# The output projection of a gated expert layer as seven block products instead of eight

## The chip, the cores and the metric

The kernel runs on one core of a Trainium2 chip. The metric is device time in microseconds (us), the median over several executions; beside it stands one profiled execution, whose trace the rows below are taken from.

## The reference, cut to what matters

Windowed attention (4 batches, 8 heads, 512 local and 32 global tokens, head size 64) gives 2176 token rows of 512 features. Two expert layers follow, and the change is in the last matrix product of the second:

```python
def _moe_ref(x, w1, w2, w3, w_out):
    h = np.maximum(np.maximum(x @ w1, x @ w2), x @ w3)
    return (h @ w_out).astype(np.float32)

def _moe2_ref(x, w_gate, w_val, w_out):       # x 2176 x 512, w_gate and w_val 512 x 1536
    gate = 1.0 / (1.0 + np.exp(-(x @ w_gate)))
    val = x @ w_val
    return (gate * val @ w_out).astype(np.float32)   # w_out 1536 x 512
```

## The kernel before, in words

**Stages.** The first 400 us are attention with the first expert layer woven in. From about 450 to 697 us the products x @ w_gate and x @ w_val run ("layer 3"), and from 697 us to the end the product with w_out ("layer 4").

**Number format.** Each f32 operand of layers 3 and 4 is split into a high half (rounded by a cast on ACT) and a low half (the rest, a subtraction on DVE). A product is the sum of three matmuls, high x high, high x low and low x high (`TERMS`), so each pair of 128-row blocks costs three matmuls on PE, each with its own weight load.

**Layer 3** already works with seven products instead of eight. For each gate or value matrix, each pair of 128 output columns (`j`) and each of three groups of tokens (`PAIRS`, twice 384, 384 or 320 tokens) there is a unit of seven products, `l3_prod(u, k)`. Products 1, 6, 7 and 4 add into one PSUM bank ("a"), with copies of it taken by ACT between them (`snap`); products 5 and 3 share a second bank ("e"), product 2 has a third ("b"). `l3_out` adds a bank and a copy on DVE. The order on PE is 1, 5, (4 of the unit before), 6, 2, (3 of the unit before), 7, so the copies have time while PE does another product. The gated result goes to DRAM as `gd`, feature blocks by tokens, through SP's DMA queue (L1051).

**Layer 4.** `wo_pre` (six times during layer 3) loads two 128-row blocks of w_out, brings them to f32 and stores them in DRAM (`wod`). Near the end of layer 3, as places in SBUF come free, `wo_prep` loads the twelve blocks and splits them. `g_prep(i)` loads the 1536 x 128 block of `gd` for token tile i (768 KB) and splits it in two pieces of 768 columns, a cast (L1089) and a subtraction (L1091) each. `moe2_l4(i, f)` issues the 12 x 3 matmuls of 512 columns of tile i into one bank, with the tokens' block as the stationary operand (L1102), and `moe2_out` copies the bank out and stores it. There are 17 tiles, 612 matmuls. Tile 0 runs before products 4 and 3 of the last layer 3 unit (the two "leftover" products), tiles 1 to 16 after them.

**Order.** Each step is a generator; every `yield` is a place where other work may stand. All steps are numbered events, and the list `ORDER` at the head of the file says in which order they are issued. Each engine, and SP's queue of DMA issues, takes its own instructions strictly in that order; the framework adds the waits. Places in SBUF are given by hand (`mem(at, ...)`), so a load into a place waits until what was there has been used.

## Time and profile before

| what | us |
|---|---|
| median of 3 runs | 845.67 (844.76 to 848.22) |
| the profiled execution | 843.73 |
| its span, first to last instruction | 842.0 |
| tile 0 of layer 4 on the chain | 697.85 to 706.04 |
| tiles 1 to 16 of layer 4 on the chain | 707.79 to 838.39 |

PE is TensorE's matmuls, PEld its weight loads (they overlap matmuls), DVE is VectorE, ACT ScalarE, POOL GpSimd, SPq the queue of DMA issues. L1102 is line 1102 of the kernel. In a row of a group, "x612 | 139.1, 389" means 612 instructions, 139.1 us busy in union, 389 ns from start to end of one; matmuls are pipelined, so the spacing of their starts is less than that length. "[0.35 <-ACT sn L1030]" means that the engine was idle for 0.35 us before, until that instruction.

### The profile page before, as it was taken

The page shows a single profiled execution, that of the slowest core. Times are in us where ns is not written, and L with a number is a line of the kernel's source. Part 1 is how long each engine was busy: PE and PEld are TensorE (multiplying, and loading weights), DVE is VectorE, ACT ScalarE, POOL GpSimd, SP SyncE. Part 2 cuts the span into 40 slices and gives each one's busy share as a digit, 9 for nine tenths or more (in the row PEclk, how much of TensorE's full clock was granted, in tenths as well). Part 3 has the DMA queues.
Part 4 walks back from the last instruction along what each step waited for, and adds up shares of the span by engine and source line. Part 5 has one row for each costly group of instructions (what it writes and reads, how often), then busy time and mean ns, then how long its engine had stood idle before and what let it go on. Part 6 is the DMA issues. An engine that isn't in the chain of part 4 may idle for free.

```text
span 842.0 us, 17071 instructions
## 1 busy us (share of the span) xinstructions
PE 815.9 (97%) x6422; PEld 744.4 (88%) x6422; DVE 529.8 (63%) x1200; ACT 452.1 (54%) x1112; POOL 148.5 (18%) x149
## 2 busy tenths in 40 slices
PE   6899699999999999999999999999999999999998
PEld 4678589898999988899999999999999998888886
DVE  3979767756676666864686887867766575222210
ACT  4986466746555565564456656556655453222220
POOL 3142245334232332323220000000000000000000
PEclk9999899999999999999999999999999999999999
DMA  9977346544453455444435244646442286445320
GB/s 208 273 182 190 86 79 115 88 88 97 95 108 80 78 114 104 89 94 82 153 124 191 97 159 144 223 153 192 164 146 77 72 256 196 130 122 147 108 70 37
DMA packets 224706, 109.72 MB, mean 130 GB/s; under 512 B 160752, under 2 KB 209392, under 8 KB 224624
## 3 DMA queue, kind: packets, MB, share of 16 engines
q1 hardware_dynamic: 221968, 107.98, 48.6%
q8 instruction: 50, 0.82, 0.4%
q10 hardware_dynamic: 2656, 0.66, 0.4%
q14 instruction: 32, 0.26, 0.1%
HBM read 71.76 MB, written 25.43 MB: 115 GB/s over the span
## 4 chain that ended last, share of the span: by engine, by line
PE 85%; DVE 5%; DMA 4%; SPq 2%; ACT 2%; issue 1%; POOL 0%; POOLq 0%; DVEq 0%; ACTq 0%
PE pa L1024 17%; PE acc L1102 16%; PE ps L320 10%; PE ps L322 9%; PE ps L321 9%; PE pe L1024 8%; PE pb L1024 4%; PE sp L612 3%; PE ot L766 2%; PE ps L904 2%; PE sg L629 1%; DMA m<-in_moe_w_dram 1%; DMA m<-in_v_l_dram 1%; PE ps L868 1%; PE og L835 1%
## 5 line engine op out<-in xcount | busy, mean ns | idle before, releaser
L1024 PE MATMUL pa<-m,m 128*128 128x384 f32 (+1 forms) x864 | 155.1, 327 | 0.3 <-ACT sn L1030 0.3
L320 PE MATMUL ps<-xt,m 128*128 128x288 f32 (+1 forms) x504 | 149.1, 296 | 2.1 <-DVE h L882 1.9
L322 PE MATMUL ps<-xt,m 128*128 128x288 f32 (+1 forms) x504 | 146.8, 291 | 0.0
L1024 PEld LDWEIGHTS pa<-m,m 128*128 128x128 f32 x864 | 144.4, 188 | 0.9 <-ACT sn L1030 0.8
L321 PE MATMUL ps<-xt,m 128*128 128x288 f32 (+1 forms) x504 | 144.9, 288 | 0.0
L1102 PE MATMUL acc<-m,m 128*128 128x512 f32 x612 | 139.1, 389 | 0.0
L1102 PEld LDWEIGHTS acc<-m,m 128*128 128x128 f32 x612 | 114.8, 188 | 23.7
L320 PEld LDWEIGHTS ps<-xt,m 128*128 128x128 f32 x504 | 94.7, 188 | 10.0 <-issue 4.3
L321 PEld LDWEIGHTS ps<-xt,m 128*128 128x128 f32 x504 | 94.8, 188 | 0.0
L322 PEld LDWEIGHTS ps<-xt,m 128*128 128x128 f32 x504 | 94.6, 188 | 0.0
L1091 DVE TENSOR_TENSOR m<-m,m 128x768 fp32r<-128x768 f32 x34 | 32.4, 958 | 87.5 <-ACT m L1089 87.5
L1030 ACT COPY sn<-pa 128x384 f32<-128x384 f32 (+1 forms) x108 | 49.7, 461 | 64.8 <-PE pa L1024 64.7
L1024 PE MATMUL pe<-m,m 128*128 128x384 f32 (+1 forms) x432 | 83.1, 327 | 0.0
L1089 ACT CAST m<-m 128x768 fp32r<-128x768 f32 x34 | 28.5, 840 | 83.9 <-PE acc L1102 71.7
L1024 PEld LDWEIGHTS pe<-m,m 128*128 128x128 f32 x432 | 72.8, 188 | 0.3 <-DVE m L1006 0.3
L647 ACT ACTIVATE sm<-sm,st 128x224 f32<-128x224 f32 x128 | 60.9, 479 | 11.0 <-DVE st L618 10.9
L882 DVE TENSOR_TENSOR h<-ps,h 128x288 f32<-128x288 f32 (+1 forms) x90 | 39.0, 437 | 43.6 <-PE ps L322 36.7
L270 POOL TENSOR_TENSOR h<-h,h 128x288 fp32r<-128x288 f32 (+1 forms) x42 | 41.4, 988 | 97.1 <-ACT h L887 93.1
L693 DVE TENSOR_TENSOR pc<-sm,pc 64x512 f16<-64x512 f32 (+1 forms) x72 | 51.8, 719 | 6.6 <-ACT pc L690 5.7
L618 DVE CUSTOM_DVE_ANT_0 sm<-sp,mask 128x224 f32<-128x224 f32 x128 | 43.8, 385 | 12.5 <-PE sp L612 9.8
L320 PE MATMUL ps<-h,m 128*128 128x288 f32 (+1 forms) x168 | 50.4, 300 | 0.0
L321 PE MATMUL ps<-h,m 128*128 128x288 f32 (+1 forms) x168 | 48.5, 289 | 0.6 <-POOL h L270 0.6
(162 smaller groups left out, 1436.0 us busy)
## 6 DMA issues: line engine op xcount, KB each, us to landing
m<-gd SPq DMA_DIRECT2D x17, 768.0 KB, 5.1
m<-in_moe_w_dram SPq DMA_DIRECT2D x18, 512.0 KB, 5.9
gd<-sgt SPq DMA_DIRECT2D x48, 192.0 KB, 1.9
m<-in_moe_w_val_dram SPq DMA_DIRECT2D x6, 1024.0 KB, 5.2
wr<-in_moe_w_out_dram SPq DMA_DIRECT2D x6, 1024.0 KB, 6.5
m<-in_moe_w_gate_dram SPq DMA_DIRECT2D x5, 1024.0 KB, 5.1
vr<-in_v_l_dram SPq DMA_DIRECT2D x48, 96.0 KB, 2.4
out_dram<-m SPq DMA_DIRECT2D x17, 256.0 KB, 2.4
```

The costliest lines, as they stand in the source:

```text
L270: nc.gpsimd.tensor_tensor(out=out, in0=a, in1=f32(b), op=ALU.subtract)
L320: nc.tensor.matmul(ps, lhsT=wh, rhs=xh, start=first, stop=False)
L321: nc.tensor.matmul(ps, lhsT=wh, rhs=xl, start=False, stop=False)
L322: nc.tensor.matmul(ps, lhsT=wl, rhs=xh, start=False, stop=last)
L618: nc.vector.tensor_tensor_reduce(out=sm[:, hh, j], in0=sp[hh][:, j, 0:224], in1=mask[:, half + j, :], scale=-SC, scalar=3.0e38, op0=ALU.ad ...
L647: nc.scalar.activation(sm4[:, i], sm4[:, i], AF.Exp, bias=st[:, 0, i:i + 1], scale=-1.0, accum_out=st[:, 2, i:i + 1])
L693: nc.vector.tensor_tensor(out=l_, in0=s_, in1=h_, op=ALU.subtract)
L882: nc.vector.tensor_tensor(out=a, in0=ps[:, 0:n], in1=a, op=ALU.max)
L1024: nc.tensor.matmul(ps, lhsT=w[l][:, a, i], rhs=x[m][:, i], start=(k in (1, 2, 5) and i + l + m == 0), stop=(k in (2, 3, 4) and i == 1 and ...
L1030: nc.scalar.copy(t[:, 0:n], pend[u]["a"][:, 0:n])
L1091: nc.vector.tensor_tensor(out=lo, in0=a, in1=f32(hi), op=ALU.subtract)
L1102: nc.tensor.matmul(acc[i], lhsT=t[l][:, f % 6], rhs=w[m], start=(f == 0 and l + m == 0), stop=(f == NF2 - 1 and l == 1))
```

## The change

Tile 0 (tokens 0 to 127) stays as it is, 36 matmuls of 512 columns. The other 2048 tokens are taken in 8 blocks of 256. A block's operand is four quarters (A11, A12, A21, A22: first or second half of the 1536 features by first or second 128 tokens), and w_out is four quarters of 768 x 256 (B11, B12, B21, B22). Seven products replace eight, with the sums S1 = A21 + A22, S2 = S1 - A11, S3 = A11 - A21, S4 = A12 - S2 on the tokens' side and T1 = B12 - B11, T2 = B22 - T1, T3 = B22 - B12, T4 = B21 - T2 on the weights'. Each product is 6 x 3 matmuls of 256 columns (`l4_prod`). Banks, copies, the order of the products and the output sums are those of layer 3 (`snap4`, `out4`), over the same PSUM tiles; in the last block 7 stands before the 3 of the block before.

`wo_pre` now loads one 128-row block of each half of w_out, makes the four sums (four subtractions of 256 columns on DVE) and stores them in DRAM (`wot`, two stores more). At the end of layer 3, `wo_prep` loads and splits the plain weights in six pieces of 1024 columns, and `wt_prep` the sums in four of 1536 columns. `g_first` loads and splits tile 0 in two halves. `g_prep(i)` loads 1536 x 256 of `gd` (1.5 MB, into one of three places), makes four sums of 768 columns on DVE and seven casts and seven low halves of 768 columns; for the halves of each of the seven operands there is one place, which all blocks share. `out4` makes three sums of 256 columns on DVE and one copy on ACT for each block, each with a store of 128 KB.

The new `ORDER` is the same up to the first event of layer 3. Around the first tile it has, on DVE: low half of tile 0's first half, low A11 of block 0 as the tile starts, the layer 3 outputs that are ready, low half of tile 0's second half, S1, S3, S2, low S1, low T4, low T3 (while tile 0 and the leftover products run), the last layer 3 outputs, low S2 (during product 1 of block 0), low A12, low S3, low A11 of block 1, low A22, S4 of block 0, S1 of block 1, low S4, S3 and S2 of block 1, an output sum, low S1 of block 1. On ACT, the casts stand in the same order, those of T4 and T3 between the casts of S1 and S2 of block 0. On SP's queue: three loads of plain weights (512 KB each), T2, two more loads of plain weights, tile 0's first half, block 0, tile 0's second half, and with the last products of layer 3 T4, T3 and block 1, with the stores of `gd` between.

```diff
@@ ORDER, lines 114 to 194 @@
...
@@ -261,7 +261,8 @@
     dram = ctx.enter_context(tc.tile_pool(name="dram", bufs=1, space=bass.MemoryType.DRAM))
     x2d = [dram.tile([KD, P, NT], F32, tag="x2d", name="x2d")]
     gd = dram.tile([NF2, P, NT], F32, tag="gd", name="gd")
-    wod = dram.tile([NF2, P, DM], F32, tag="wod", name="wod")
+    wod = dram.tile([P, 2, NF2 // 2, DM], F32, tag="wod", name="wod")
+    wot = dram.tile([P, 4, NF2 // 2, 256], F32, tag="wot", name="wot")
 
     def f32(ap):
         return ap.bitcast(F32)
@@ -1052,61 +1053,183 @@
         yield
 
     wo = {}
+    AJ, AT = (R0, R0 + 6144), (R0 + 12288, 7168, 0, 18432)
+    AGR, AO = (10240, 21504), 6144
+    AG = {A11: 16384, S1: 14848, S2: 13312, A12: 24576, S3: 3072, A22: 4608, S4: R0 + 15360}
 
     def wo_pre(i):
+
         raw = sg_pool.tile([P, 2 * DM, 2], I32, tag="wr", name="wr", bufs=1)
-        nc.sync.dma_start(out=raw.rearrange("p (f d) t -> p f (d t)", f=2),
-                          in_=w_out2[2 * i * P:(2 * i + 2) * P, :].rearrange("(f p) d -> p f d", p=P))
+        nc.sync.dma_start(out=raw.rearrange("p (h d) t -> p h (d t)", h=2),
+                          in_=w_out2.rearrange("(h f p) d -> f p h d", h=2, p=P)[i])
         yield
         c = mem(AST, (2 * DM,), I32)
         yield from to_f32(raw, True, out=c)
         yield
-        nc.sync.dma_start(out=wod[2 * i:2 * i + 2].rearrange("f p d -> p f d"), in_=f32(c).rearrange("p (f d) -> p f d", f=2))
-        yield
-
-    def wo_prep(f):
-        at = R0 + 1024 * f if f < 10 else AO2 + 1024 * (f - 10)
-        v = mem(at + DM, (DM,))
-        nc.sync.dma_start(out=v, in_=wod[f])
-        yield
-        hi = mem(at, (DM,), F32R)
+        c = f32(c).rearrange("p (h d) -> p h d", h=2)
+        nc.sync.dma_start(out=wod[:, 0:2, i], in_=c)
+        b11, b12, b21, b22 = c[:, 0, 0:256], c[:, 0, 256:512], c[:, 1, 0:256], c[:, 1, 256:512]
+        t12, t34 = mem(R0 - 8704, (2, 256)), mem(R0 - 512, (2, 256))
+        tt = nc.vector.tensor_tensor
+        tt(out=t12[:, 0], in0=b12, in1=b11, op=ALU.subtract)
+        yield
+        tt(out=t12[:, 1], in0=b22, in1=t12[:, 0], op=ALU.subtract)
+        yield
+        tt(out=t34[:, 0], in0=b22, in1=b12, op=ALU.subtract)
+        yield
+        tt(out=t34[:, 1], in0=b21, in1=t12[:, 1], op=ALU.subtract)
+        yield
+        for n, t in enumerate((t12, t34)):
+            nc.sync.dma_start(out=wot[:, 2 * n:2 * n + 2, i], in_=t)
+        yield
+
+    def split(at, src, n):
+
+        v = mem(at[1], (n,))
+        nc.sync.dma_start(out=v, in_=src)
+        yield
+        hi = mem(at[0], (n,), F32R)
         nc.scalar.copy(hi, v)
         yield
-        lo = mem(at + DM, (DM,), F32R)
+        lo = mem(at[1], (n,), F32R)
         nc.vector.tensor_tensor(out=lo, in0=v, in1=f32(hi), op=ALU.subtract)
-        wo[f] = hi, lo
-        yield
+        return hi, lo
+
+    def wo_prep(h, j):
+        at = AJ[h] + 1024 * j
+        v = yield from split((at, at + 3072), wod[:, h, 2 * j:2 * j + 2].rearrange("p f d -> p (f d)"), 1024)
+        wo[h, j] = [x.rearrange("p (f d) -> p f d", f=2) for x in v]
+        yield
+
+    def wt_prep(n):
+        v = yield from split((AT[n], AT[n] + 1536), wot[:, n].rearrange("p f d -> p (f d)"), 1536)
+        wo[(T1, T2, T3, T4)[n]] = [x.rearrange("p (f d) -> p f d", f=6) for x in v]
+        yield
+
+    def wo_op(op, f, m):
+
+        if op in wo:
+            return wo[op][m][:, f]
+        h, d = {B11: (0, 0), B21: (1, 0), B22: (1, 1)}[op]
+        return wo[h, f // 2][m][:, f % 2, 256 * d:256 * d + 256]
 
     gt = {}
 
+    def g_first(h):
+
+        raw = mem(AG[(S2, S1)[h]], (6, P))
+        nc.sync.dma_start(out=raw, in_=gd[6 * h:6 * h + 6, :, 0:P].rearrange("f p t -> p f t"))
+        yield
+        if h == 0:
+            t = sg_pool.tile([P, 2, 6, P], F32R, tag="wr", name="g0", bufs=1)
+        else:
+            t = mem(AG[S2], (2, 6, P), F32R)
+        nc.scalar.copy(t[:, 0], raw)
+        yield
+        nc.vector.tensor_tensor(out=t[:, 1], in0=raw, in1=f32(t[:, 0]), op=ALU.subtract)
+        gt[h] = t
+        yield
+
     def g_prep(i):
-        raw = mem(AXR + 1536 * (i % 2), (NF2, P))
-        nc.sync.dma_start(out=raw, in_=gd[:, :, i * P:(i + 1) * P].rearrange("f p t -> p f t"))
-        yield
-        for h in range(2):
-            a = raw[:, 6 * h:6 * h + 6]
-            hi, lo = (mem(7168 + 3072 * (i % 3) + 1536 * h + 768 * m, (6, P), F32R) for m in range(2))
-            nc.scalar.copy(hi, a)
-            yield
-            nc.vector.tensor_tensor(out=lo, in0=a, in1=f32(hi), op=ALU.subtract)
-            gt[i, h] = hi, lo
-            yield
+
+        if i % 3 < 2:
+            raw = mem(AGR[i % 3], (NF2, 2, P))
+        else:
+            raw = sg_pool.tile([P, 2, NT], F32, tag="sgt", name="graw", bufs=1).rearrange("p a t -> p (a t)")
+            raw = raw[:, 0:NF2 * 2 * P].rearrange("p (f h t) -> p f h t", f=NF2, h=2)
+        t0 = P + 256 * i
+        nc.sync.dma_start(out=raw.rearrange("p f h t -> p f (h t)"), in_=gd[:, :, t0:t0 + 256].rearrange("f p t -> p f t"))
+        yield
+        a11, a12, a21, a22 = raw[:, 0:6, 0], raw[:, 6:12, 0], raw[:, 0:6, 1], raw[:, 6:12, 1]
+        tt = nc.vector.tensor_tensor
+        s1 = mem(AG[S1] + 768, (6, P))
+        src = {A11: a11, S1: s1, S2: a11, A12: a12, S3: a21, A22: a22, S4: a22}
+
+        def high(op):
+            hi = mem(AG[op], (6, P), F32R)
+            nc.scalar.copy(hi, src[op])
+            gt[i, op] = hi, mem(AG[op] + 768, (6, P), F32R)
+
+        def lows(op):
+            hi, lo = gt[i, op]
+            tt(out=lo, in0=src[op], in1=f32(hi), op=ALU.subtract)
+
+        high(A11)
+        yield
+        lows(A11)
+        yield
+        tt(out=s1, in0=a21, in1=a22, op=ALU.add)
+        yield
+        high(S1)
+        tt(out=a21, in0=a11, in1=a21, op=ALU.subtract)
+        yield
+        tt(out=a11, in0=s1, in1=a11, op=ALU.subtract)
+        yield
+        lows(S1)
+        yield
+        for op in (S2, A12, S3, A22):
+            high(op)
+            yield
+            lows(op)
+            yield
+        tt(out=a22, in0=a12, in1=a11, op=ALU.subtract)
+        yield
+        high(S4)
+        yield
+        lows(S4)
+        yield
 
     acc = {}
 
-    def moe2_l4(i, f):
+    def l4_first(f):
         if f == 0:
-            acc[i] = ps_mm.tile([P, DM], F32, tag="mm", name="acc")
-        t, w = gt[i, f // 6], wo[f]
+            acc[0] = ps_mm.tile([P, DM], F32, tag="mm", name="acc")
+        t, w = gt[f // 6], wo[f // 6, f % 6 // 2]
         for l, m in TERMS:
-            nc.tensor.matmul(acc[i], lhsT=t[l][:, f % 6], rhs=w[m], start=(f == 0 and l + m == 0),
+            nc.tensor.matmul(acc[0], lhsT=t[:, l, f % 6], rhs=w[m][:, f % 2], start=(f == 0 and l + m == 0),
                              stop=(f == NF2 - 1 and l == 1))
 
-    def moe2_out(i):
-        o = mem(DM * (i % 3), (DM,))
-        nc.scalar.copy(o, acc.pop(i))
-        yield
-        nc.sync.dma_start(out=out[i * P:(i + 1) * P, :], in_=o)
+    def first_out():
+        o = mem(AO, (DM,))
+        nc.scalar.copy(o, acc.pop(0))
+        yield
+        nc.sync.dma_start(out=out[0:P, :], in_=o)
+        yield
+
+    def l4_prod(i, k):
+        a, b = PROD[k]
+        s = pend.setdefault(i, {})
+        if k == 1:
+            s["a"] = ps_mm.tile([P, DM], F32, tag="mm", name="pa")
+        elif k == 2:
+            s["b"] = ps_b.tile([P, DM], F32, tag="pb", name="pb", bufs=2)
+        elif k == 5:
+            s["e"] = ps_b.tile([P, DM], F32, tag="pe", name="pe", bufs=3)
+        ps = s["b" if k == 2 else "e" if k in (5, 3) else "a"][:, 0:256]
+        g = gt[i, a]
+        for f in range(6):
+            for l, m in TERMS:
+                nc.tensor.matmul(ps, lhsT=g[l][:, f], rhs=wo_op(b, f, m), start=(k in (1, 2, 5) and f + l + m == 0),
+                                 stop=(k in (2, 3, 4) and f == 5 and l == 1), skip_group_check=True)
+
+    def snap4(i, what):
+        t = pend[i][what] = rb.tile([P, CH], F32, tag="sn", name="sn", bufs=5)
+        nc.scalar.copy(t[:, 0:256], pend[i]["a"][:, 0:256])
+
+    n_out = [0]
+
+    def out4(i, t, d):
+        s = pend[i]
+        o = mem(AO + 256 * (n_out[0] % 4), (256,))
+        n_out[0] += 1
+        if (t, d) == (1, 0):
+            nc.scalar.copy(o, s["a"][:, 0:256])
+        else:
+            bank, other = {(0, 0): ("b", "s1"), (1, 1): ("e", "s3"), (0, 1): ("e", "s2")}[t, d]
+            nc.vector.tensor_tensor(out=o, in0=s[bank][:, 0:256], in1=s[other][:, 0:256], op=ALU.add)
+        yield
+        r = P + 256 * i + P * t
+        nc.sync.dma_start(out=out[r:r + P, 256 * d:256 * d + 256], in_=o)
         yield
 
 
@@ -1216,13 +1339,13 @@
             units += [(0, j, 0), (0, j, 1), (1, j, 0), (1, j, 1), (0, j, 2), (1, j, 2)]
         else:
             units += [(q, j, p) for q in range(2) for p in range(3)]
-    tm, ended, began, t_l4 = T_B, {}, {}, [0] * (NT // P)
-    D4 = 36 * .234
+    tm, ended, began = T_B, {}, {}
+    D4 = 36 * .228
     for i in range(len(units) + 1):
         this = units[i] if i < len(units) else None
         prev = units[i - 1] if i else None
         if this is None:
-            t_l4[0] = tm
+            t_l4 = tm
             tm += D4
         for v, k in ((this, 1), (this, 5), (prev, 4), (this, 6), (this, 2), (prev, 3), (this, 7)):
             if v is None:
@@ -1231,7 +1354,24 @@
             once(("l3", *v, k), tm, l3_prod, v, k)
             tm += 6 * (PAIRS[v[2]][1] + 32) / 2400
             ended[v, k] = tm
-    t_l4[1:] = [tm + D4 * i for i in range(NT // P - 1)]
+    N4 = NT // 256
+    e4 = {}
+    for i in range(N4 + 1):
+        this, prev = (i if i < N4 else None), (i - 1 if i else None)
+        seq = [(this, 1), (this, 5), (prev, 4), (this, 6), (this, 2), (prev, 3), (this, 7)]
+        if i == N4 - 1:
+            seq[5:] = [(this, 7), (prev, 3)]
+        for v, k in seq:
+            if v is None:
+                continue
+            once(("p4", v, k), tm, l4_prod, v, k)
+            tm += 18 * .12
+            e4[v, k] = tm
+    for i in range(N4):
+        for k, what in ((1, "s1"), (6, "s2"), (7, "s3")):
+            once(("s4", i, what), e4[i, k] + .2, snap4, i, what)
+        for t, d, t0 in ((0, 0, e4[i, 2] + .25), (1, 1, e4[i, 7] + .7), (1, 0, e4[i, 4] + .2), (0, 1, e4[i, 3] + .25)):
+            put(("o4", i, t, d), steps(t0, 0, .6), out4(i, t, d))
     for v in units:
         for k, what in ((1, "s1"), (6, "s2"), (7, "s3")):
             once(("sn", *v, what), ended[v, k] + .2, snap, v, what)
@@ -1257,19 +1397,33 @@
             free[place] = go + 7.5
         put(("w7", q, j), first + steps(go, *(.1, .45, .45, .45, .45, .6, .6, .8, .6, 1.2)), w_prep(q, j, buf, place))
     for i in range(NF2 // 2):
-        put(("wo", i), steps(490.0 + 28 * i, 0, 9.0, 1.2, 1.2, 1.3, 1.3), wo_pre(i))
+        put(("wo", i), steps(490.0 + 28 * i, 0, 9.0, 1.2, 1.2, 1.3, 1.3, .5, .5, .5, .5), wo_pre(i))
 
     v0 = ended[(1, NF2 // 2 - 1, 0), 3]
     v1 = ended[(1, NF2 // 2 - 1, 1), 3]
+    for h in range(2):
+        for j in range(3):
+            put(("wop", h, j), steps(v0 + .3 + 3 * h + j, 0, 4.0, 1.2), wo_prep(h, j))
+    v2 = ended[(0, NF2 // 2 - 1, 2), 3] + .1
+    for n in range(4):
+        put(("wt", n), steps((v0 + 9, v1 + 1, v2, e4[0, 1] - 2)[n], 0, 5.0, 1.5), wt_prep(n))
+    for h in range(2):
+        put(("g0", h), steps(v1 - 1 + h, 0, 3.5, .9), g_first(h))
+    for i in range(N4):
+        t0 = e4[i, 1] - 2.2
+        if i == 0:
+            ld = v1 + 1.5
+            tc4 = [max(ld + 5, t0 - 3) + .1 * k for k in range(3)] + [t0 - 2.5 + .1 * k for k in range(3)] + [t0 - 1.6, t0 - 1.5] + [t0 + .3 + .8 * k for k in range(9)]
+        else:
+            ld = max(t0 - 22, e4[0, 1] - 2)
+            tc4 = [t0 + x for x in (-9, -8.2, -7.4, -6.6, -5.8, -5, -4.2, -3.4, -2.6, -1.8, .3, 1.1, 6.8, 7.6, 8.4, 13.4, 14.2)]
+            if i == 1:
+                tc4 = [x + 4 if x < t0 else x for x in tc4]
+                tc4 = [max(x, ld + 5 + .6 * k) for k, x in enumerate(tc4)]
+        put(("gp", i), [ld, *tc4], g_prep(i))
     for f in range(NF2):
-        put(("wop", f), steps(v0 + .3 + 1.1 * f, 0, 4.0, .8), wo_prep(f))
-    for i in range(NT // P):
-        t0 = t_l4[i]
-        ld, cv = max(t0 - 18, v0 + 3.4 + i), max(t0 - 9, v1 + .5 + .1 * i)
-        put(("gp", i), steps(ld, 0) + steps(cv, 0, .9, .2, .9), g_prep(i))
-        for f in range(NF2):
-            once(("l4", i, f), t0 + D4 * f / NF2, moe2_l4, i, f)
-        put(("out", i), steps(t0 + D4, .1, .7), moe2_out(i))
+        once(("l4", f), t_l4 + D4 * f / NF2, l4_first, f)
+    put(("out",), steps(t_l4 + D4, .1, .7), first_out())
 
     order = [e[1] for e in sorted(ev, key=lambda e: e[:2])] if ORDER is None else ORDER
     assert sorted(order) == list(range(len(ev)))
```

## Rows read from the trace of the kernel before

**Rows 1.** Page, part 1 (busy) and part 4 by line, whole span.

```profile
PE 815.9 (97%) x6422; PEld 744.4 (88%) x6422; DVE 529.8 (63%) x1200; ACT 452.1 (54%) x1112; POOL 148.5 (18%) x149
...
PE pa L1024 17%; PE acc L1102 16%; PE ps L320 10%; PE ps L322 9%; PE ps L321 9%; PE pe L1024 8%; PE pb L1024 4%; PE sp L612 3%; PE ot L766 2%; PE ps L904 2%; PE sg L629 1%; DMA m<-in_moe_w_dram 1%; DMA m<-in_v_l_dram 1%; PE ps L868 1%; PE og L835 1%
```

**Rows 2.** Busy by stretch: PE, weight loads, DVE, ACT, POOL, granted clock, DMA share, GB/s.

```profile
413.27:417.54 4.27, 4.27 (x39) 4.27 (x38) 4.27 (x6) 3.02 (x6) 1.07 (x1) 1.00 0.09 31
450.00:685.00 235.00, 235.00 (x1415) 234.48 (x1415) 170.05 (x289) 139.12 (x261) 0.00 (x0) 1.00 0.46 155
706.91:838.39 131.48, 131.47 (x583) 108.64 (x581) 28.99 (x32) 31.35 (x44) 0.00 (x0) 1.00 0.39 113
```

**Rows 3.** Chain in order of time, 690 to 842: start, length, what.

```profile
697.85 8.19 PE acc L1102 x36
...
706.91 0.88 PE pe L1024 x6
707.79 130.60 PE acc L1102 x576
...
838.46 0.59 ACT m L1107
```

**Rows 4.** Timeline of PE, 256-column stretch: start, length; first and next after last.

```profile
413.27 0.28 PE L320 MATMUL ps<-h,m 128*128 128x256 f32 x1
...
417.54 0.29 PE L320 MATMUL ps<-xt,m 128*128 128x288 f32 x1
```

**Rows 5.** Groups by line and form, 690 to 842, low halves and casts.

```profile
L1091 DVE TENSOR_TENSOR m<-m,m 128x768 fp32r<-128x768 f32 x34 | 32.4, 958 | 87.5 <-ACT m L1089 87.5
L1089 ACT CAST m<-m 128x768 fp32r<-128x768 f32 x34 | 28.5, 840 | 83.9 <-PE acc L1102 71.7 <-DMA m<-gd 12.1
```

**Rows 6.** Groups by line and form, 400 to 842, DVE and ACT.

```profile
L1030 ACT COPY sn<-pa 128x320 f32<-128x320 f32 x36 | 15.3, 426 | 24.4 <-PE pa L1024 24.4
...
L1006 DVE TENSOR_TENSOR m<-m,m 128x1024 fp32r<-128x1024 f32 x12 | 14.7, 1224 | 0.3
...
L1043 DVE TENSOR_TENSOR sgt<-pe,sn 128x320 f32<-128x320 f32 x12 | 5.8, 485 | 1.0 <-ACT sn L1030 1.0
...
L994 DVE TENSOR_TENSOR m<-m,m 128x256 f32<-128x256 f32 x11 | 4.6, 417 | 0.0
...
L952 DVE TENSOR_TENSOR m<-m,m 128x768 f32<-128x768 f32 x2 | 1.9, 954 | 0.7 <-DMA m<-x2d 0.7
```

**Rows 7.** Timeline, 683 to 698, PE and ACT: start, length, idle before.

```profile
685.27 1.04 PE L1024 MATMUL pe<-m,m 128*128 128x320 f32 x6
...
691.79 1.04 PE L1024 MATMUL pe<-m,m 128*128 128x320 f32 x6
...
694.43 0.83 ACT L1089 CAST m<-m 128x768 fp32r<-128x768 f32 x1 [0.86 <-DMA m<-gd]
...
696.22 0.43 ACT L1030 COPY sn<-pa 128x320 f32<-128x320 f32 x1
...
696.70 1.15 PE L1024 MATMUL pa<-m,m 128*128 128x320 f32 x6 [0.35 <-ACT sn L1030]
...
697.69 0.63 PE L1102 MATMUL acc<-m,m 128*128 128x512 f32 x2
```

**Rows 8.** Busy by stretch, for the last two columns, DMA.

```profile
683.50:694.40 10.90, 10.90 (x73) 10.90 (x72) 8.00 (x15) 5.42 (x11) 0.00 (x0) 1.00 0.85 257
690.00:693.00 3.00, 3.00 (x23) 3.00 (x22) 1.61 (x3) 1.55 (x5) 0.00 (x0) 1.00 1.07 326
404.00:406.00 2.00, 2.00 (x19) 2.00 (x18) 0.00 (x0) 0.40 (x1) 0.66 (x1) 1.00 1.05 415
```

**Rows 9.** Waits, 450 to 842: us in total, times, longest.

```profile
ACT sn L1030 <- PE pa L1024: 64.7, 69, 2.7
```

**Rows 10.** DMA issues by line: count, KB each, us to landing.

```profile
out_dram<-m SPq DMA_DIRECT2D x17, 256.0 KB, 2.4
...
gd<-sgt SPq DMA_DIRECT2D x24, 160.0 KB, 2.1
```

156 rows, old and new, of the table ORDER are left out of this document.

## The prediction

> **What bounds the kernel now.** The page comes first: part 1 shows PE busy for 97% of the span, and part 4, the chain of waits by line, begins with PE lines, 16% of it on line 1102, the line that the change replaces [rows 1]. A share over the whole span mixes stages, so the busy times by stretch come next. From 706.91 to 838.39, the 16 token tiles in question, PE is busy for 131.47 of 131.48 us at full granted clock, weight loads for 83% of it, DVE for 29 us, ACT for 31 us [rows 2]. The chain in order of time agrees: 130.60 us of back-to-back matmuls, 576 of them, with nothing between [rows 3]. Each 512-column matmul takes 130.60/576 = 226.7 ns, and only fewer or cheaper matmuls shorten the stage. In the third layer (450 to 685) PE is also busy all the time, with DVE at 170 of 235 us [rows 2]: anything added there is free as long as PE's inputs stay ahead.
>
> **The change, part by part.** *Products.* 576 matmuls of 512 columns go. Each of the 8 blocks of 256 tokens has 7 products of 6 x 3 matmuls at 256 columns, 1008 in all. The price of one stands in the trace: in the second layer of the first expert stage, 36 matmuls of the same number format, 128x128 by 256 columns, each with its own weight load, start at 413.27 and the next work starts at 417.54 [rows 4], so 4.27/36 = 118.6 ns. (The 280 ns in those rows is the latency of a pipelined matmul; the spacing is what counts.) 1008 x 118.6 = 119.6 us against 130.6: **-11.0 us**. Not 1/8 (-16.3, the end if 256 columns cost half of 226.7, 114.3 us), because two halves cost 10.5 ns more than a whole. The other end is the weight load: 108.64 us for 581 loads is 187 ns of busy time each [rows 2], and 1008 x 187 = 188.5 us would be +57.9. But in the stretch from 413.27 weight loads are busy for all 4.27 us, 38 of them [rows 2], while matmuls start every 118.6 ns: loads overlap each other, so their busy time is no spacing. I take 118.6.
>
> The Trainium skill, page "TensorE: Matmul & The Clock Gate", section "Back-to-back issue gap", says that the spacing in a real stream is set by weight load and matmul together, and gives a sustained 131 ns at 512 columns and 81 ns at 128. A straight line between these makes 98 ns at 256, and the estimate from that page is 576 x 131 = 75 us before and 1008 x 98 = 99 us after: the change would lose 23 us. The trace disagrees at both points (226.7 and 118.6 ns), and its ratio of 1.91 decides.
>
> *Supply in the steady rounds.* A block takes 7 x 18 x 118.6 ns = 14.9 us of PE. DVE gets 7 low halves and 4 sums of 768 columns at 958 ns [rows 5] (a plain f32 sum of that size takes 954 [rows 6]) and 3 output sums of 256 columns, about 0.42 us each by the 417 ns of a 256-column sum [rows 6]: 11 x 0.958 + 1.3 = 11.8 us. ACT gets 7 casts at 840 ns [rows 5], and 3 snapshots and a copy of 256 columns, below the 426 ns of 320 [rows 6]: at most 7.6 us. Both fit under 14.9, and the operands of one block are made while the block before is multiplied, so I cost them at nothing. Were the cover gone, each round would be as long as its supply (a rival below). Loads are the same 12 MB, in 1.5 MB pieces every 14.9 us, 105 GB/s; the stage moves 113 GB/s now [rows 2].
>
> *The crossing.* Here the change adds most, in little time. From the start of the first tile to the third matmul of block 1's product 5, PE has 8.2 us for the tile, two leftover products at 0.88 [rows 3] and six products of 18 x 0.1186 = 2.13: 22.8 us. By the new order DVE has to get through this before: 10 low halves (A11, S1, S2, A12, S3, A22, S4 of block 0, the second half of tile 0, A11 and S1 of block 1) and 7 sums at 0.958, 16.3 us; the low halves of T3 and T4 at 1536 columns, for which 954 to 1224 ns from 768 to 1024 [rows 6] extrapolates to 1.76 each, 3.5 us; some seven layer 3 outputs at 0.49 [rows 6], 3.4 us; one output sum, 0.4. That is 23.6 us in 22.8, and each hand-over from an ACT cast is a chance to wait. From there on DVE gains 3 us a round and catches up. ACT stands in line too: the casts of A11, T3 and T4 wait for loads, and behind them on ACT wait snapshots that PE needs. What wait for that now is seen: the cast at 694.43 waited 0.86 us for a load, the snapshot at 696.22 stood behind it, PE began its next product at 696.70 with 0.35 idle, and the first tile began at 697.69 [rows 7], 0.6 us after the 697.07 that six products of 0.88 us from 691.79 would give. In the new order the only cast of the tile's tokens ahead of that snapshot is of tile 0's first half, whose load is asked for some 8 us before, so I count 0.6 back. For the DVE queue and late loads I take 1.5, with ends 0 and 6: the load of block 0 (1.5 MB) stands in the order near the product at 685.27 [rows 7], behind 1 MB of weights asked for some 2 us earlier and 0.4 MB of tile 0, with 5 stores of 192 KB (0.9 MB) among them. That is 3.9 MB from about 683.5; at the 326 GB/s of 512-byte pieces, or the 415 of larger ones [rows 8], it lands at 693 to 695.5, in time for a cast at 696; at the 257 GB/s of this same stretch now [rows 8] it lands at 698.7, some 3 late, and the T3 and T4 loads behind it as late again. Crossing: 1.5 - 0.6 = **+0.9** (-0.6 to +6).
>
> *Weight sums in layer 3.* 24 DVE subtractions of 256 columns at 417 ns [rows 6] are 10.0 us, and 12 more stores stand in SP's queue ahead of the gated outputs' stores. DVE has 65 us idle in the stretch, and ACT waited on PE for snapshots 64.7 us in 69 waits [rows 9], the sign that PE's inputs are ahead. Ends 0 and 10.0; I take **+0.3**, near the row that shows the cover.
>
> *End.* From the last matmul's end at 838.39 to the span's end at 842.0 are 3.6 us: a copy of 0.59 [rows 3] and a 256 KB store (2.4 us to landing [rows 10]). After: a sum of 0.42 and a 128 KB store, a 160 KB one taking 2.1 [rows 10]: **-0.5** (-0.7 to 0).
>
> Sum: -11.0 + 0.9 + 0.3 - 0.5 = -10.3. The profiled execution took 843.73 us (span 842.0 and 1.73 around it), the median of three runs is 845.67, 1.94 above it. I expect a span of 831.7, a profiled time of 833.4, and on the median's scale 845.67 - 10.3 = **835.4 us**.
>
> **Rivals.** *A, the crossing is bound by loads:* loads of block 0, T3, T4 and block 1 come late one after another, ACT stands at them and PE waits the 6 us above instead of 1.5: 4.5 more, 839.9; with a late block 1 besides, 842. For: the DMA engines are at a share of 0.85 there now, 1.07 at the peak [rows 8], and more is asked of them. Against: most of the added bytes travel in pieces of 1 KB and more, and 415 GB/s were had of those.
> *B, layer 3 loses its cover:* the subtractions stand in DVE's queue ahead of sums that free PSUM, and up to 10.0 us come back on PE: 845, no change. For: DVE is 72% busy there. Against: PE lost nothing in 235 us.
> *C, slower: single operand buffers make casts and low halves a serial chain.* Each of the seven operands of a block has one place, so a cast waits for the product of the block before, its low half for the cast, and queues in order carry the wait on. Wholly serial, a round takes 7 x (0.84 + 0.96) + 4 x 0.96 + 1.3 = 17.7 us instead of 14.9: 8 x 2.8 = +22, 857. It decides from 130.6/8 = 16.3 us a round. For: DVE's low halves waited 87.5 us for the casts in the stage of now [rows 5], though with nothing else to do. Against: any operand has some 12 us from the end of its last use to its next, and DVE has other sums in between.
> *D, a fixed price of a matmul:* if the weight load sets the pace in this stage, 187 ns each, the time is 845.67 + 57.9 = 904. The stretch at 413 speaks against it.
>
> **How the numbers follow.** About 0.5% (4.2 us) is what a measurement can tell from no change: faster is below 841.4, slower above 849.9. My case 0.68; A 0.14 (0.09 faster, 0.05 same); B 0.07 (0.05 same, 0.02 slower with its waits added up); C 0.09, slower; D 0.02, slower. Faster 0.68 + 0.09 = 0.77, same 0.10, slower 0.13. The low end of the range is every term at its good end, -11.0 - 0.6 - 0.7 = -12.3, so 833.4, less 0.9 for the scatter of a median (844.76 to 848.22 before): 832.5. The high end takes in A, 842. What is left out is B's end, C and D.
>
> **What would show it.** Right: the new product lines fill PE from the leftover products to the end, 119.6 us for 1008 matmuls at about 118.6 ns, PE idle in the crossing below 2 us, layer 3 still without PE idle, rounds of 14.9 us. Wrong: rounds above 15.5 with PE waiting for DVE's low halves (C), PE waiting in the first two rounds and ACT for loads (A), PE idle on snapshots or output sums from 450 to 685 (B), matmuls 180 ns apart (D).

## The result and the profile after

The changed kernel takes 837.56 us (median of 4 runs, 836.84 to 837.76), against 845.34 (844.76 to 848.22) for the kernel before beside it: -7.8 us, a ratio of 0.99 (95% interval 0.9876 to 0.9923). Five more rounds of the same two kernels gave 836.39 against 845.8: -9.4 us, 0.9888 (0.9874 to 0.9903). The forecast was 835.4, 10.3 us below its own median.

The page of the changed kernel, parts 1 and 4 by line, answers to [rows 1]:

```profile
PE 809.5 (97%) x6854; PEld 759.3 (91%) x6854; DVE 602.7 (72%) x1302; ACT 477.9 (57%) x1150; POOL 148.0 (18%) x149
...
PE pa L1025 17%; PE ps L321 10%; PE ps L323 9%; PE ps L322 9%; PE pe L1025 8%; PE pa L1212 8%; PE pe L1212 4%; PE pb L1025 4%; PE ps L869 3%; PE sp L613 3%; PE pb L1212 2%; PE ot L767 2%; PE ps L905 2%; PE sg L630 2%; PE acc L1189 1%
```

Line 1102's 16% are gone; the product line 1212 has 8 + 4 + 2 = 14% in their place. DVE's share rises from 63 to 72%, and PE stays at 97%. Busy by stretch (PE, weight loads, DVE, ACT, POOL, clock, DMA share, GB/s), answering to [rows 2]:

```profile
452.00:687.00 235.00, 234.81 (x1412) 233.97 (x1411) 176.07 (x305) 138.70 (x254) 0.00 (x0) 1.00 0.52 170
710.32:831.29 120.97, 120.95 (x1009) 120.75 (x1007) 86.67 (x109) 52.15 (x84) 0.00 (x0) 1.00 0.36 118
```

Both stretches are still full of PE work at full granted clock. In the second, 1008 matmuls take 120.97 us, 120.0 ns each, and DVE is busy for three times as long as before in that stage (86.67 us, 28.99 before) without PE waiting for it. In the third layer DVE is 6 us busier than before. PE's waits from 460 to the end are all in these two rows (waits of the changed kernel: us in total, times, longest):

```profile
PE pe L1025 <- ACT m L1194: 0.4, 1, 0.4
PE pa L1025 <- ACT sn L1031: 0.2, 1, 0.2
```

The chain of the changed kernel in order of time (start, length, what; [rows 3] for before) places them:

```profile
669.16 1.48 ACT m L1092
670.64 0.38 ACT sn L1031
671.02 0.04 issue
671.07 2.35 PE pa L1025 x12
...
699.62 8.31 PE acc L1189 x36
707.92 0.89 PE pa L1025 x6
708.81 0.02 issue
708.84 0.59 ACT m L1194
709.43 0.04 issue
709.48 0.85 PE pe L1025 x4
710.32 2.16 PE pa L1212 x18
712.48 2.16 PE pe L1212 x18
...
829.12 2.17 PE pe L1212 x18
831.29 0.02 issue
831.31 0.42 DVE m L1229
```

At 669.16 ACT casts T1, the first sum of weights, at 1.48 us; the snapshot that PE needs stands behind it. At 708.84 ACT copies tile 0's result, and the second leftover product waits for that copy, which it doesn't read. Past that, products of 18 x 120 = 2160 ns follow each other without a gap.

**Where the 6.0 us between the two spans went** (842.0 and 836.0). By the first starts on PE and the end of the last matmul:

| part | before | after | difference | forecast |
|---|---|---|---|---|
| up to the start of layer 3 | 448.80 | 450.66 | +1.86 | 0 |
| layer 3 to the first tile | 248.89 | 248.80 | -0.09 | } +1.2 |
| first tile to the first product | 9.94 | 10.70 | +0.76 | } |
| the 16 tiles | 130.76 | 121.13 | -9.63 | -11.0 |
| last matmul to the end of the span | 3.61 | 4.71 | +1.10 | -0.5 |

The first row is ahead of anything changed. Stretches at half the granted clock lie there in both profiles and are longer in this execution; one of them, busy by stretch, in the kernel before:

```profile
95.00:107.00 12.00, 8.41 (x28) 6.74 (x29) 6.07 (x13) 3.12 (x12) 1.49 (x1) 0.72 0.07 16
```

and in the changed kernel:

```profile
95.00:107.00 12.00, 7.83 (x19) 5.92 (x20) 6.65 (x14) 2.65 (x9) 1.49 (x1) 0.57 0.11 24
```

The mean granted clock is 0.72 and 0.57 of full speed (1.2 GHz for part of the time, 2.4 for the rest). That is not all of it: in the second profile of the changed kernel (c_after, below) it is 0.72 there too, and layer 3 begins at 450.67 all the same. But e3_halves, which up to there is the kernel before, also begins it at 450.67. Over the profiles of all the kernels here, layer 3 began anywhere from 447.7 to 452.5, so I take this row as scatter of one execution, not as a cost of the change. The profiled execution of the kernel before was a short one besides: its span is 842.0, and the seven executions of the second measurement have 841.8 to 844.8, in the median 844.1.

The last row has a cause of its own. DMA of the changed kernel from 831.5 to the end (a queue with packets, MB and share; then the store with its KB and us to landing):

```profile
q8 instruction: 1, 0.02, 2.0%
...
out_dram<-m SPq DMA_DIRECT2D x1, 128.0 KB, 3.2
```

One load of 16 KB of instructions begins at 832.38, takes 1.41 us of a DMA engine that also carries a part of the last store, and the store lands after 3.2 us: eight of its packets of 1 KB start only from 833.77 on, as that load ends, all the others before 833.2. In the profile of the second measurement the code load comes after the store, and the store takes 1.7 us. SP's wait for it, changed kernel, first measurement:

```profile
SPq L1462 <- DMA out_dram<-m: 2.9, 1, 2.9
```

and the second:

```profile
SPq L1462 <- DMA out_dram<-m: 1.4, 1, 1.4
```

There the end is 3.36 us, 0.25 less than before. Without the two parts that differ between executions, the change is worth -0.09 + 0.76 - 9.63 - 0.25 = -9.2 us, beside -9.4 between the medians of the second measurement.

Groups by line and form, changed kernel, 700 to 836 (busy us, mean ns, idle before), answering to [rows 5, 6]:

```profile
L1212 PE MATMUL pa<-m,m 128*128 128x256 f32 x576 | 72.0, 283 | 0.0
...
L1155 DVE TENSOR_TENSOR m<-m,m 128x768 fp32r<-128x768 f32 x44 | 41.5, 956 | 17.9 <-ACT m L1150 17.1
...
L1229 DVE TENSOR_TENSOR m<-pe,sn 128x256 f32<-128x256 f32 x16 | 6.8, 422 | 8.8 <-PE pe L1212 5.9 <-ACT sn L1217 2.9
```

The durations taken from before hold within about 1% on DVE: a low half 956 ns (958), an output sum 422 (417 assumed). The matmul's own 283 ns says as little of the spacing as the 280 before.

### The profile page after: what moved, and what is told of

It reads as the page before. It is cut to its first block, busy times and chain, and to the rows that moved or that the text cites. A ratio compares the mean times of both kernels' runs of the same rounds, so it can differ in the third digit from the quotient of the medians.

```text
span 836.0 us, 18171 instructions
## 1 busy us (share of the span) xinstructions
PE 809.5 (97%) x6854; PEld 759.3 (91%) x6854; DVE 602.7 (72%) x1302; ACT 477.9 (57%) x1150; POOL 148.0 (18%) x149
## 4 chain that ended last, share of the span: by engine, by line
PE 88%; DVE 4%; ACT 3%; DMA 2%; issue 1%; SPq 1%; POOL 0%; POOLq 0%; ACTq 0%; DVEq 0%
PE pa L1025 17%; PE ps L321 10%; PE ps L323 9%; PE ps L322 9%; PE pe L1025 8%; PE pa L1212 8%; PE pe L1212 4%; PE pb L1025 4%; PE ps L869 3%; PE sp L613 3%; PE pb L1212 2%; PE ot L767 2%; PE ps L905 2%; PE sg L630 2%; PE acc L1189 1%
## 5 line engine op out<-in xcount | busy, mean ns | idle before, releaser
L1025 PEld LDWEIGHTS pa<-m,m 128*128 128x128 f32 x864 | 144.5, 188 | 0.8 <-ACT sn L1031 0.7
L1212 PE MATMUL pa<-m,m 128*128 128x256 f32 x576 | 72.0, 283 | 0.0
L1212 PEld LDWEIGHTS pa<-m,m 128*128 128x128 f32 x576 | 70.4, 192 | 0.0
L1150 ACT CAST m<-m 128x768 fp32r<-128x768 f32 x44 | 36.6, 836 | 44.1 <-PE pa L1212 13.9
L1155 DVE TENSOR_TENSOR m<-m,m 128x768 fp32r<-128x768 f32 x44 | 41.5, 956 | 17.9 <-ACT m L1150 17.1
```

The lines of the kernel that those rows point to most:

```text
L1025: nc.tensor.matmul(ps, lhsT=w[l][:, a, i], rhs=x[m][:, i], start=(k in (1, 2, 5) and i + l + m == 0), stop=(k in (2, 3, 4) and i == 1 and ...
L1155: tt(out=lo, in0=src[op], in1=f32(hi), op=ALU.subtract)
L1212: nc.tensor.matmul(ps, lhsT=g[l][:, f], rhs=wo_op(b, f, m), start=(k in (1, 2, 5) and f + l + m == 0), stop=(k in (2, 3, 4) and f == 5 and ...
```

## The experiments

### The same kernel again (c_after)

> The changed kernel once more, as the mark for e2. Theory (span differences of single profiles come from the stretch before layer 3, whose code is the same): start of layer 3 to start of the first tile again 248.8 us, 1008 products 121.0 us, while the start of layer 3 may move by 1 to 2 us with the granted clock. The last store again lands late if a code load falls on it every time (4.7 us from the last matmul to the end of the span); rival (chance): about 3.3 us there. Ratio to the kernel before 0.99.

Measured: 836.39 us, -9.4; start of layer 3 at 450.67, layer 3 248.82, tile to products 10.72, products 121.13, end 3.36. Layer 3, crossing and products repeat to 0.03 us; the long end doesn't, and in the profiles of e2, e5 and e8 to e11 it is 3.2 to 3.3 us, which makes it chance.

### Two places and one order (e2_two_places)

```
-        o = mem(AO, (DM,))          # first_out, tile 0's result
+        o = mem(R0 - 512, (DM,))
 ORDER: ..., 3209, 2216, 2828, 3213, 2217, ...   (was 3209, 3213, 2216, 2828, 2217)
```

3213 is ACT's cast of T1, 2828 the snapshot behind it.

> The copy of tile 0's result goes to a place that shares nothing with layer 3's weights, and the cast of T1 stands behind a snapshot instead of ahead of it. Theory (the two waits of PE in the crossing come from these two): the wait of 0.4 us in leftover product 3 and the one of 0.2 us at the end of layer 3's second group are gone, first tile to first product 10.0 us instead of 10.7, layer 3 0.3 us shorter, in all 0.8 to 1.2 us faster than the changed kernel. Rival (the crossing is bound by DVE's queue and loads): the waits come back one product later and the sum changes by less than 0.3 us.

Its chain, 690 to 712:

```profile
695.33 0.88 PE pa L998 x6
696.21 8.31 PE acc L1162 x36
704.52 0.88 PE pa L998 x6
705.39 0.88 PE pe L998 x6
706.27 2.16 PE pa L1185 x18
```

No ACT piece stands between the leftover products any more. Layer 3 takes 248.33 us (-0.47), tile to products 10.06 (-0.64): both waits came from the order and the place that these two edits change, and nothing took their place. (The edits were not run apart; which one took which wait away is read from the instruction that each wait names.) So the copy of tile 0 held PE up through the place it wrote to, not through data: it writes elements 6144 to 6656, where the low halves of S1 and S2 of the same unit's weights had lain, and the product reads S4 beside them, no byte of these. The time is 834.91 (832.23 to 836.01), 1.5 below c_after; the runs overlap, so by the times alone this is not shown, by the traces it is.

### Twelve kinds of 36 matmuls (e1_spacing)

Behind the last product stand 12 sets of 36 matmuls, each with its own weight load, whose results nobody reads. Widths, banks, repeated operands and starts differ from set to set:

```
+        sets = [(256, 256, 256, 18, 0, 0), (256, 256, 256, 36, 0, 0), (256, 0, 256, 36, 0, 0), ...
+                nc.tensor.matmul(ps[:, dst:dst + n], lhsT=y[l][:, ws * f:ws * f + P],
+                                 rhs=x[k][:, off + rs * f:off + rs * f + n], ...
```

> Behind the last product, 12 sets of 36 matmuls on operands that lie still: 256 columns in two banks of 18; in one bank; same moving operand each time; same weights each time; moving operand off by 7 elements; second half of the bank; then 248, 224, 128, 288, 384, 512 columns. Theory (spacing is columns plus 32 cycles at 2.4 GHz, wherever operands lie): 120.0 ns in all 256-column sets, then 116.7, 106.7, 66.7, 133.3, 173.3, 226.7. Rival 1 (bank changes or places cost the 1.4 ns over 118.6): one of the 256-column sets falls to 118.6 or below. Rival 2 (weight loads set a floor): 224 or 128 columns stay above their value. The kernel is longer by about 60 us.

Four of the sets (busy by stretch; a set is a stretch, its length over 36 the spacing): 256 columns with the same weights each time; 256 with the moving operand 7 elements off; 224; 128:

```profile
844.73:849.05 4.32, 4.32 (x38) 4.32 (x37) 0.00 (x0) 0.00 (x0) 0.00 (x0) 1.00 0.00 0
849.05:853.28 4.23, 4.23 (x38) 4.23 (x37) 0.00 (x0) 0.00 (x0) 0.00 (x0) 1.00 0.00 0
861.73:865.74 4.01, 4.01 (x39) 4.01 (x37) 0.00 (x0) 0.00 (x0) 0.00 (x0) 1.00 0.00 0
865.74:869.72 3.98, 3.98 (x39) 3.98 (x37) 0.00 (x0) 0.00 (x0) 0.00 (x0) 1.00 0.00 0
```

| columns | 128 | 224 | 248 | 256 | 256, moving operand off by 7 | 288 | 384 | 512 |
|---|---|---|---|---|---|---|---|---|
| ns | 110.5 | 111.4 | 115.0 | 120.0 | 117.5 | 133.2 | 173.9 | 227.8 |

From 256 columns up the spacing is within 1.2 ns of (N + 32)/2.4, so two halves pay those 32 columns twice. Below, it stops falling near 110 ns. One bank or two, the same moving operand or the same weights each time: 120.0; the second half of a bank: 119.5. What moved it by more at 256 columns was the start of the operand (and its step, 248 in that set), so neither banks nor repetition explains the 118.6 of the forecast.

### The old products in halves (e3_halves)

```
-                nc.tensor.matmul(acc[i], lhsT=t[l][:, f % 6], rhs=w[m], ...
+            for d in (0, 256):
+                nc.tensor.matmul(acc[i][:, d:d + 256], lhsT=t[l][:, f % 6], rhs=w[m][:, d:d + 256], ...
```

This is the kernel before, its 512-column matmuls of all 17 tiles cut in two: the thin matmuls without Strassen's scheme.

> The kernel before, each 512-column matmul of layer 4 as two of 256 columns (1224 instead of 612), all else the same: the thin matmul alone, without the seventh less work. Theory (120.0 ns each): layer 4 takes 146.9 instead of 138.7 us, +8.2. By 118.6 ns: +6.4. Rival (a fixed price per matmul, weight loads of 187 ns): +90. The change's gain is then 1/8 of 138.2 less the 7.6 that thin matmuls cost on 16 tiles.

Its chain:

```profile
700.01 8.63 PE acc L1103 x72
...
710.41 138.25 PE acc L1103 x1152
```

138.25/1152 = 120.0 ns. Halving costs 138.25 - 130.60 = 7.65 us on the 16 tiles. The gain can now be split by measured parts: seven products instead of eight are worth 138.25/8 = 17.3 us, the thinner shape takes back 7.65, which leaves 9.6.

### Where 120.0 comes from (e6_places, e7_places2)

Again sets of 36 whose results nobody reads, all 256 columns wide. The starts of the moving operand's high and low half and of the weights are shifted by so many 4-byte elements:

```
+        sets = [(0, 0, 0, 256), (16, 16, 0, 256), (0, 0, 16, 256), (16, 16, 16, 256), ...
+                nc.tensor.matmul(ps[:, 0:256], lhsT=y[l][:, 256 * f + ow:256 * f + ow + P], rhs=x[k][:, o:o + 256], ...
```

> Twelve sets of 36 matmuls of 256 columns behind the last product, by shifts in elements of the moving operand's high half, its low half, the weights, and the step between blocks: (0,0,0,256), (7,7,0,256), (0,0,0,248), (0,7,0,256), (0,0,7,256), (7,7,7,256), (1,1,0,256), (8,8,0,256), (16,16,0,256), (64,64,0,256), (128,128,0,256), (32,0,0,256). Theory A (where the moving operand begins decides): all sets with a shifted moving operand between 116 and 119 ns, the first and the fifth 120.0. Theory B (the step of 248 decides, not the start): only the third below 120. Theory C (what decides is the distance between weights and moving operand): the fifth falls too and the sixth goes back to 120.

| moving high, low, weights | 0,0,0 | 7,7,0 | 0,7,0 | 0,0,7 | 7,7,7 | 1,1,0 | 8,8,0 | 16,16,0 | 32,0,0 | 64,64,0 | 128,128,0 |
|---|---|---|---|---|---|---|---|---|---|---|---|
| ns | 120.0 | 116.9 | 116.2 | 116.7 | 117.4 | 123.0 | 116.9 | 113.4 | 119.0 | 119.9 | 120.0 |

A twelfth set, unshifted with steps of 248 instead of 256 elements, ran at 118.5. Shifting the weights does as much as shifting the moving operand, 64 and 128 elements do nothing, 1 makes it worse. Shifting both by 7 should have led back to 120 if the distance alone counted, and gave 117.4. None of the three theories passes whole.

> Twelve more sets of 36 matmuls of 256 columns, shifts in elements of moving high, moving low, weights: (0,0,0), (16,16,0), (0,0,16), (16,16,16), (0,0,48), (0,0,32), (12,12,0), (24,24,0), (32,32,0), (48,48,0), (16,0,0), (0,16,0). Theory A (the moving operand's own start decides): the second and the fourth about 113.4, sets 3, 5 and 6 at 120. Theory C (the distance between the weights' start and the moving operand's decides): the fourth at 120, the third and fifth below 117 like the second. Either way a shift that reaches 113.4 would be worth 1008 x 6.6 ns = 6.6 us in the kernel.

Four of its sets (busy by stretch): nothing shifted; weights by 16; both by 16; moving by 48:

```profile
831.21:835.53 4.32, 4.32 (x38) 4.32 (x37) 0.42 (x1) 0.00 (x0) 0.00 (x0) 1.00 0.10 32
839.77:843.86 4.09, 4.09 (x38) 4.09 (x37) 0.00 (x0) 0.00 (x0) 0.00 (x0) 1.00 0.00 0
843.86:848.17 4.31, 4.31 (x39) 4.31 (x38) 0.00 (x0) 0.00 (x0) 0.00 (x0) 1.00 0.01 4
869.52:873.60 4.08, 4.08 (x38) 4.08 (x37) 0.00 (x0) 0.00 (x0) 0.00 (x0) 1.00 0.00 0
```

4.32/36 = 120.0, 113.6, 119.7 and 113.3 ns. Here the distance of the two starts decides, counted modulo 64 elements: both shifted by 16 is as slow as none; weights on by 16 and moving on by 48, the same distance, give 113.6 and 113.3; moving on by 16 and weights on by 48, the same again, 117.9 and 117.7; 32 either way 118.7 and 118.6. (Moving on by 12 gave 118.2, by 24 119.9; one half alone by 16, 118.9 and 117.8.) But the set (16,16,0), at 117.9 in this kernel, had run at 113.4 in the one before. Two values for one set of places: what picks between them is open (the two kernels ran on different chips, which no run here separates). And (7,7,7) had run at 117.4 there, not at 120. That the distance matters is shown, the exact rule is not.

The Trainium skill, page "TensorE: Matmul & The Clock Gate", section "Step-by-step: what each phase is for", says that the streaming operand and the weight load have SBUF read ports of their own, so that loading the next weights takes no read bandwidth from the matmul that runs. With that alone a shift of the weights would change nothing; the trace has 120.0 and 113.6 ns for it.

### Three times the weight sums (e4_sums_x3)

```
+        for _ in range(3):
             tt(out=t12[:, 0], in0=b12, in1=b11, op=ALU.subtract)      # and so for all four
```

The 24 subtractions of layer 3 are each done three times, with the same result: 48 x 0.417 = 20.0 us more on DVE.

> Each of the 24 weight sums of layer 3 made three times: 20 us more DVE work in the 248.8 us between the start of layer 3 and the first tile. Theory (DVE has cover there): 248.8 to 250, PE idle below 1 us more. Rival B (the sums stand ahead of work that PE needs): at least 5 us of the 20 on PE, 254 to 269.

Layer 3's start to the first tile takes 260.07 us instead of 248.8, +11.3; the time is 850.55. My theory failed, rival B was right of this size. Waits of PE in this kernel:

```profile
PE pa L1025 <- ACT sn L1031: 6.0, 8, 1.4
PE pe L1025 <- DVE tm L1044: 1.1, 2, 0.9
```

and busy by stretch in the middle of the layer:

```profile
550.00:600.00 50.00, 45.73 (x268) 43.59 (x267) 47.09 (x90) 27.22 (x49) 0.00 (x0) 1.00 0.59 192
```

DVE is at 47 of 50 us there, PE loses 4.3. A mean share of 72% had left room for 10 us of sums and not for 30: the sums stand close together where they are, so the room where they stand counts and not the 65 us of the whole layer.

### The low halves twice (e5_lows_x2)

```
+            for _ in range(1 if op == S1 else 2):
                 tt(out=lo, in0=src[op], in1=f32(hi), op=ALU.subtract)
```

Six of the seven low halves of each block are computed twice, with the same result, which makes DVE's work 17.1 us a block against PE's 15.1.

> Six of the seven low halves of each block made twice: DVE gets 11.3 + 6 x 0.96 = 17.1 us a round of 15.1. Theory (DVE is covered up to the round's 15.1 us and then sets it): rounds of about 17.1 us, 8 products stages longer by some 14 us, less what the first blocks and the last round spare, so 10 to 16. Rival C (cast and low half run as a serial chain, the rounds are already near it): 6 x 0.96 come on top of nearly every round, more than 30 us. If DVE still had cover by running ahead: below 5.

The 16 tiles take 137.27 us, +16.1, at the upper end of what was expected; the time is 853.02. Three stretches in this kernel, the first of 15 us, the others of 17:

```profile
715.00:730.00 15.00, 10.55 (x81) 10.14 (x80) 14.71 (x17) 5.06 (x9) 0.00 (x0) 0.88 0.54 171
747.00:764.00 17.00, 17.00 (x144) 17.00 (x144) 16.59 (x21) 6.42 (x11) 0.00 (x0) 1.00 0.36 117
798.00:815.00 17.00, 15.30 (x127) 15.10 (x127) 16.59 (x21) 6.62 (x11) 0.00 (x0) 1.00 0.38 124
```

DVE is busy for 14.71 of 15 and 16.59 of 17. PE loses 4.5 us in the first of these stretches, nothing in the second, and 1.7 a round later. Meanwhile the granted clock fell to half (1.2 GHz) twice, for 6.8 us from 726.3, in the midst of a wait of PE, and for 3.4 us from 774.1, just after one, so not all of the 16.1 us is waiting. The length of a round holds all the same: after its long waits PE starts again at 773.94, 791.02, 808.08 and 825.15, 17.07 us apart, and the round with 3.4 us at half clock is as long as the others. The rounds become as long as DVE's work and no longer: a chain of casts, low halves and products one after the other (rival C) would have cost over 30. In the changed kernel that means some 4 us of room a round.

### Places in the kernel itself (e8_shift16, e9_shift0, e10_shift48, e11_shift8)

```
-    AGR, AO = (10240, 21504), 6144
+    AGR, AO = (10240, 21504), (6160, 6416, 6672, 17952)
+    AG = {op: at + 16 for op, at in AG.items()}
 ORDER: T1's cast behind the snapshot, as in e2; tile 0's copy (3386) behind the leftover product (2248)
```

All places of the block operands, the stationary ones of these matmuls, move by 16 elements; the others have +0, +48 and +8 in that line (in the last two with other output places). The two waits are taken out by order alone.

> The changed kernel with the operands of the 8 blocks (the weights of its matmuls) begun 16 elements, 64 bytes, later than a multiple of 64 elements, the four places of the outputs moved to make room, the cast of T1 behind a snapshot, and the copy of tile 0's result behind the last leftover product. Theory C (the distance between the starts of weights and moving operand sets the spacing of 256-column matmuls): 113.5 ns a matmul in all seven products, 1008 of them 114.4 instead of 121.0 us; in all some 7 to 8 us faster than the changed kernel, about 828.5, DVE's 11.3 us still inside rounds of 14.3. Theory A (the moving operand's own start) : 120.0 as before, only the 1.1 us of the two moves. Rival (what holds with engines idle doesn't hold beside DVE's and ACT's traffic): between 115 and 120 with scatter.

> The same kernel with a shift of 0, the mark for e8_shift16. Theory: 120.0 ns a matmul, 121.0 us for the products, 1.1 us faster than the changed kernel (the two waits in the crossing gone), about 835.2. Rival: the copy of tile 0's result now waits for the leftover product and holds up ACT's casts of block 0, so that a wait comes back in the first round and less than 0.5 us is won.

> As e8_shift16 with a shift of 48 elements. With still operands, sets whose moving operand lay 16 behind the weights (modulo 64) ran at 113.4, 117.7 and 117.9 ns, those with 16 ahead of it (as e8) at 113.3 and 113.7, while e8's products ran at 117.8 throughout. Theory (the distance has two steady spacings, and which one is taken is not decided by the distance alone): 113.4 or 117.8 in all products, one value throughout. Rival (the distance alone decides, other steps between blocks shift it): a third value.

> As e8_shift16 with a shift of 8 elements, which with still operands gave 116.9 ns with scatter from 113 to 120 (and 7 elements on the weights 116.7). Theory: 116 to 117.5 with scatter, products 117.5 us, about 1 us faster than e8_shift16. Rival (what was measured with still operands does not carry over, as 113.4 did not): 117.8 or more.

The products with +16, busy by stretch:

```profile
708.37:827.01 118.64, 118.64 (x1009) 118.58 (x1007) 87.06 (x110) 53.47 (x86) 0.00 (x0) 1.00 0.37 120
```

and with +0:

```profile
708.84:829.81 120.97, 120.97 (x1009) 120.81 (x1007) 88.27 (x110) 53.33 (x86) 0.00 (x0) 1.00 0.37 119
```

| | +0 | +8 | +16 | +48 |
|---|---|---|---|---|
| ns a matmul | 120.0 | 118.3 | 117.8 | 117.8 |
| us, median | 835.13 | 833.61 | 832.71 | 832.74 |
| ratio (95%) | 0.9884 (0.9867 to 0.9901) | 0.9871 (0.9856 to 0.9886) | 0.9857 (0.9839 to 0.9875) | 0.9858 (0.9817 to 0.99) |

Only places differ between +0 and +16, and 2.33 us go, 2.4 in the medians; 6.6 had been expected of the products. The 113.4 ns that the loose sets had with a shift of 16 didn't appear, nor their 116.9 with 8: the kernel took 117.8 and 118.3 from the first product to the last. The chip doesn't explain that: e7 and e8 ran on the same one, and weights on by 16 gave 113.6 there in a loose set. e8 has one wait that e9 hasn't, outside the products, and e11 has the same (0.4 us):

```profile
PE pa L998 <- ACT sn L1004: 0.3, 1, 0.3
```

In both, the chain goes over low halves and layer 3 outputs in DVE's queue, the store of a gated result and the load of tile 0's first half (8.13 us) to its cast on ACT, and the snapshot behind that cast holds PE up.

With +16, 832.71 (832.08 to 833.68) beats both kernels: 12.8 us below the kernel before in the same rounds, where c_after had been 9.4 below it.

## Why the prediction was right, and where it was off

The mechanism and the sign were right: the product lines fill PE to the end, no round waits for its supply, layer 3 keeps its cover, and none of the rivals A to D happened. The 837.56 lies in the range. Of 10.3 us forecast, 9.2 are found in the parts that the change touches, by its terms:

- **Products, -11.0 forecast, -9.6 measured: the mis-sized term.** I took 118.6 ns from 4.27 us of 36 matmuls in another stage [rows 4] as the price of a 256-column matmul. It is no constant, though the trace of the kernel before showed no other value: the 19 stretches of 21 or more such matmuls in that stage (166 to 418 us) all run at 118.3 to 118.7. Why that stage has this value no run here shows. The stretch's single starts lay 113 to 125 ns apart; the new products ran at 120.0 throughout, and e8 against e9 shows that the places of the operands alone move it by 2.2 ns, 2.3 us. Bounds were there to be had: the spread inside those 4.27 us, times 1008, was 12 us.
- **Crossing, +0.9 forecast with a DVE queue of 23.6 us in 22.8, and weight sums, +0.3: +0.67 together measured, for other reasons.** The 0.6 of the old snapshot's stall [rows 7] came back as forecast in the two profiles of this kernel, where no load and no low half was late for PE. It isn't gone for good: in e6, the same program up to its added sets, and in e8 and e11, tile 0's first load was late again, at the end of a chain over DVE's queue, and PE stood for 0.3 to 0.4 us. In the two profiles PE waited twice for ACT instead: 0.47 in layer 3 behind the cast of T1, 0.64 for a copy into a neighbouring place, each taken away by e2. The size was right by luck; the step that took 1.5 us for "the DVE queue and late loads" was wrong here.
- **Weight sums in layer 3.** At their size they cost nothing: with the two ACT waits gone the layer takes 248.33, less than the 248.89 before. The cover [rows 9] is thinner than its 64.7 us read: e4 found its end between 10 and 30 us.
- **Supply, 11.8 us of DVE in 14.9.** Measured 86.67 us in 120.97, 10.8 a round (part of the first blocks' work lies ahead of the stretch). e5 shows what lies beyond: DVE's work sets the round.
- **End, -0.5 forecast, -0.25 measured in the second profile**, +1.10 in the first with a code load beside the last store.

The ratio between a 512- and a 256-column matmul, forecast as 1.91, came out as 226.7/120.0 = 1.89. The Trainium skill, page "TensorE: Matmul & The Clock Gate", section "Back-to-back issue gap", gives a sustained 131 and 81 ns at 512 and 128 columns; the trace disagrees at both, with 227.8 and 110.5 (e1), and the loss of 23 us that the prediction had estimated from the page did not come.

## What to carry to other kernels

Price a narrower matmul by the measured spacing at that width, with the spread between its single starts as the bound, and look for the width below which it stops falling: here halves of 512 cost 7.65 us and 128 columns would cost hardly less than 224. Before trusting a mean share of an engine as cover, look at the stretch in which the added work will stand, and at what else on that queue (a long cast ahead of a short snapshot) a waiting engine needs. A wait for data that the waiting instruction doesn't read points to a place: move the place or the order and it is gone.

## What the runs showed of the hardware that I had not expected

- At 256 columns the spacing of matmuls with own weight loads depends on where the two operands start in SBUF: 113.3 to 123.0 ns over 24 sets (e6, e7). It was 120.0 with nothing shifted, 119.9 and 120.0 with the moving one on by 64 and 128 elements of 4 bytes, and 119.7 with both on by 16, but 117.4 with both on by 7.
- Below 256 columns it stops at about 110 ns (111.4 at 224, 110.5 at 128), though a weight load shows 188 to 192 ns of busy time: loads overlap each other. Whether they set that floor no run here shows, as no set ran without them.
- A load of 16 KB of instructions beside the last store made it land after 3.2 instead of 1.7 us.
